# Retention's chunks at a closer spacing, and one more half block's output product in seven products

## The chip, the cores and the metric

The kernel runs on one core of a Trainium2 chip. The metric is the device time of one execution in microseconds (us). Before the change it is 704.63 us, the median of three runs (704.38 to 705.03). The engines of the core work side by side, each on its own queue in order: TensorE (PE in the profile, with its weight loads as PEld), VectorE (DVE), ScalarE (ACT), GpSimd (POOL), and SyncE (SP), which here only starts transfers.

## The reference

Retention over 4 batches, 8 heads, 768 positions and a head size of 64, and on its result a two-layer block with `h - tanh(h)` in its middle:

```python
gamma = 1.0 - 2.0 ** (-5.0 - np.arange(H))
for t in range(S):
    state = gamma[None, :, None, None] * state + np.einsum('bhd,bhe->bhde', k[:, :, t], v[:, :, t])
    y[:, :, t] = scale * np.einsum('bhd,bhde->bhe', q[:, :, t], state)
x = y.transpose(0, 2, 1, 3).reshape(B * S, H * D)     # 3072 x 512
h = x @ w_in                                          # 3072 x 2048
out = (h - np.tanh(h)) @ w_out                        # 3072 x 512
```

## The kernel before

Retention is computed in 24 chunks of 128 positions. The two large products work on 12 half blocks of 256 tokens; the hidden width of 2048 is cut into 8 pairs of 128. A step is one half block `n` with one pair `m2`: an up product (x times w_in), the shrink `h - tanh(h)`, and, two or three steps later, that tile's output product (times w_out). There are 96 steps. The first 8 steps and chunks are in a hand-ordered opening; the loop below starts with step 8. Steps 8 to 31 are of half blocks 0 to 3; from step 32 on each half block has 8 steps in a row, half block 4 from step 32, half block 5 from step 40.

The plain products, and those in seven products (the scheme of Strassen and Winograd: seven products of quarter matrices instead of eight, with sums ahead and behind):

```python
def up(n, m2, i):                                        # L443: 8 calls of 256 columns a step
    for c in range(NC):
        nc.tensor.matmul(hp, w1[:, c, ts(2 * m2 + i, P)], xT[n // 2][:, c, ts(n % 2, TH)], ...)

def down(n, m2, j, first, last):                         # L510: 4 calls of 512 columns a step
    for i in range(2):
        nc.tensor.matmul(o_p[j], gT[n, m2][:, i, ts(j, P)], w2[:, 2 * m2 + i], ...)

def fast_up(n, m2, some):                                # L756: 14 calls of 128 columns a step
    for k in some:
        for c in range(2):
            nc.tensor.matmul(hps[n, m2][:, ts(PLACE[k], P)], s_of[m2][k - 1][:, c],
                             x_of[n][k - 1][:, c], ...)

def fast_products(n, m2, first, last, some):             # L647: 7 calls of 256 columns a step
    for k in some:
        ...
        nc.tensor.matmul(accs[n][k], left[k - 1], right, ...)
```

Each call is two instructions in the profile[...]. The sums that the seven products need are made by GpSimd: `up_weights(m2)` combines quarters of w_in, `up_tokens(n, t)` those of x, `fast_weights(m2)` those of w_out, each in four subtractions or additions, and `fast_sums(n, m2)` those of a tile's shrunk h. Their room is taken from buffers that the conversion of the weights and retention no longer need:

```python
FAST = 5                                   # output product in seven from this half block on
FAST_UP = 4                                # up product in seven from this half block on
def early_room():                          # for up_weights: raw, low, power, and one xT buffer
    ...
    yield xp.tile([P, 4 * BANK], F32, tag="xT", name="fast_x")
def later_room():                          # for fast_weights: retention's v, apart, state and kqT
    ...
```

A chunk of retention needs k and q turned. For chunks 8 and later this is done by transfers: ScalarE splits the words into `apart`, they go to DRAM, and come back transposed as `kqT`:

```python
def turn_by_dma(ci):
    apart = mid.tile([P, 2, 2, H * D], U16, tag="apart", ..., bufs=1)
    for which in range(2):
        nc.scalar.copy(out=apart[:, :, which], in_=words...)                 # L300
    rows = dram.tile([P, 2, 2 * H * D], U16, tag="rows", ...)
    nc.scalar.dma_start(out=rows, in_=apart...)                              # L303
    sides[ci] = mid.tile([P, 2, NP, P], F32, tag="kqT", ...)
    nc.sync.dma_start_transpose(out=sides[ci]..., in_=rows...)               # L305

def products(ci):
    ...  nc.tensor.matmul(..., kh[r, h], vh[r, h], ...)                      # L325, k and v
    ...  nc.tensor.matmul(..., kT[r, p, ts(a, D)], qT[r, p, ts(a, D)], ...)  # L331, needs kqT
```

A step of the loop, with the chunk that may go with it (cut):

```python
FIRST = 8
with_chunk = {BEGUN + 2 * i + 1: FIRST - 3 + i for i in range(NCH - FIRST + 3)}   # BEGUN = 8

def chunk_step(ci):
    if ci >= FIRST:
        outputs_rest(ci)                   # L379, the last part of chunk ci
        keep_x(ci)                         # its result into xT
    ...
    if FIRST <= ci + 2 < NCH:
        products(ci + 2); mask(ci + 2); state(ci + 2)
    load_chunk(ci + 4)
    if not before:
        turn_and_see(ci)                   # turn_by_dma(ci + 3), outputs(ci + 1)
    ...

for s in range(BEGUN, len(steps)):
    ...
    falls_back = s == FALL
    lag = LAG + int(s >= FALL)
    if ci is not None and not falls_back:
        chunk_step(ci)                     # ahead of the step's up product
    for i in with_weights.get(s, []):
        convert(i); load_weights(i + 3)    # weights 12 to 31, up to step 26
    if fast:
        fast_up(n, m2, (1, 5, 7, 6)); up_take(n, m2)
    else:
        for i in range(2):
            up(n, m2, i)
    if falls_back:
        chunk_step(ci)                     # behind it
    ...                                    # shrink, and the output product of an earlier tile
    if s + 1 in with_chunk:
        for which in range(2):
            scale(with_chunk[s + 1] + 3, which, nc.gpsimd)
```

So the words of chunk `ci + 3` are turned in the chunk step of `ci`, and needed by `products` in the chunk step of `ci + 1`.

Of the kernel before, what the change touches and what calls it, by code (L numbers as in the profile page):

```python
# [9 lines left out]
F32 = mybir.dt.float32  # L10
# [6 lines left out]
P = 128  # L17
# [14 lines left out]
def kernel(  # L32
# [27 lines left out]
    NP = H // 2  # L60
# [6 lines left out]
    NCH = NT // P  # L67
    BLK = 4
# [10 lines left out]
    xp = ctx.enter_context(tc.tile_pool(name="xp", bufs=NB - 1))  # L79
# [59 lines left out]
    def load_weights(i):  # L139
        if i >= NW:  # L140
            return
        dst, src = weight_ends(i)
        raw = None
        if w_out.dtype != F32:
            if EARLY <= i < EARLY + 2 * len(rooms):
                raw = rooms[(i - EARLY) // 2][:, (i - EARLY) % 2]
            else:
                raw = stage.tile([P, 2 * BANK], U32, tag="raw", name=f"raw_{i}", bufs=3)
            raws[i] = raw
        if not isinstance(src, list):  # L150
            if raw is None:
                nc.sync.dma_start(out=dst, in_=src)
            else:
                nc.sync.dma_start(out=raw, in_=src.bitcast(U32))
            return
        if raw is not None:
            dst = raw.rearrange("p (c n) -> p c n", c=NC)
        for r, k, w in src:
            nc.sync.dma_start(out=dst[r, k::2], in_=w if raw is None else w.bitcast(U32))
# [46 lines left out]
    def convert(i):  # L206
        convert_begin(i)
        convert_bits(i)
        convert_end(i, nc.gpsimd)
# [18 lines left out]
    xT = {}  # L228
# [186 lines left out]

    def keep_x(ci):
        n, nj = divmod(ci, BLK)
        if nj == 0:
            xT[n] = xp.tile([P, NP, BLK * P], F32, tag="xT", name=f"xT_{n}")

        half = xT[n][:, :, ts(nj // 2, TH)].rearrange("p (n r) t -> p r n t", r=2)
        y = y_banks[:, ci % 2][:, :: 1 - 2 * (ci % 2)]
        for odd in range(2):
            nc.scalar.copy(out=half[:, :, :, ds(P * odd + D * (nj % 2), D)],
                           in_=y[:, :, :, odd::2])
# [10 lines left out]
    def up(n, m2, i):  # L436

        if (n, m2) not in hps:
            hps[n, m2] = bank("h", f"h_{n}_{m2}")
        hp = hps[n, m2][:, ts(i, TH)]  # L440
        keep_busy(hp[:, :P])
        for c in range(NC):
            nc.tensor.matmul(hp, w1[:, c, ts(2 * m2 + i, P)], xT[n // 2][:, c, ts(n % 2, TH)],  # L443
                             start=(i == 0 and c == 0), stop=(c == NC - 1),
                             skip_group_check=True)
# [102 lines left out]

    FAST = 5
    PAIRS = NM // 2
    t_of = {}

# [27 lines left out]
    def fast_weights(m2):  # L582

        b11, b12, b21, b22 = (w2[:, 2 * m2 + i, ts(c, TH)] for i in range(2) for c in range(2))
        t = {k: next(late_room) for k in (2, 3, 4)}
        t[1] = b12
        for k, x, y in ((3, b22, b12), (1, b12, b11), (2, b22, t[1]), (4, t[2], b21)):
            nc.gpsimd.tensor_tensor(t[k], x, y, op=ALU.subtract)
        t_of[m2] = t
# [123 lines left out]
    def end_some(n):  # L713
        for _ in range(min(n, len(ending))):
            ending.pop(0)()
# [7 lines left out]
    FAST_UP = 4  # L723
# [4 lines left out]
    def up_weights(m2):  # L728

        a11, a12, a21, a22 = (w1[:, ds(2 * c, 2), ts(2 * m2 + i, P)]  # L730
                              for i in range(2) for c in range(2))
        s_ = {k: next(up_room).rearrange("p (c m) -> p c m", c=2) for k in (2, 3, 4)}
        s_[1] = a21
        for k, x, y, how in ((3, a11, a21, ALU.subtract), (1, a21, a22, ALU.add),
                             (2, s_[1], a11, ALU.subtract), (4, a12, s_[2], ALU.subtract)):
            nc.gpsimd.tensor_tensor(s_[k], x, y, op=how)
        s_of[m2] = (a11, a12, s_[4], a22, s_[1], s_[2], s_[3])
# [13 lines left out]
    def fast_up(n, m2, some):  # L751
        if 1 in some:
            hps[n, m2] = bank("h", f"h_{n}_{m2}")
# [3 lines that stand above are left out]
                                 x_of[n][k - 1][:, c], start=(k == 1 and c == 0), stop=(c == 1),  # L757
                                 skip_group_check=True)

    def up_take(n, m2):  # L760
        nc.scalar.copy(out=odd_room[0], in_=hps[n, m2])  # L761
# [20 lines left out]
    def downs(lag, half=None):  # L782

        while len(waiting) > lag:
            tile_ = waiting[0] if half == 0 else waiting.pop(0)
            if tile_[0] >= FAST:
                if tile_ == steps[-1]:
# [13 lines left out]
    BEGUN = 8  # L801
# [60 lines left out]


    FIRST = 8
    with_chunk = {BEGUN + 2 * i + 1: FIRST - 3 + i for i in range(NCH - FIRST + 3)}
    with_weights = {BEGUN: [12, 13]}
    for i in range(14, NW):
        with_weights[i - 5] = [i]
# [1 line left out]
    FIRST_UP = steps.index((FAST_UP, 0, True, False))  # L870
    FIRST_DOWN = steps.index((FAST, 0, True, False))
    FALL = FIRST_DOWN + 1
    with_sums = {}
    for m2 in range(PAIRS):
        with_sums.setdefault(FIRST_UP - 4 + m2, []).append(lambda m2=m2: up_weights(m2))
        with_sums.setdefault(FIRST_DOWN + m2, []).append(lambda m2=m2: fast_weights(m2))

    def first_tokens():
# [5 lines left out]
    def more_tokens(n):  # L884
        up_tokens(n, op.tile([P, 4 * TH], F32, tag="sum", name=f"x_{n}"))

    with_sums[FIRST_UP - 2].append(first_tokens)
    for n in range(FAST_UP + 1, 2 * NB):
        at_ = FIRST_UP + 3 + n - FAST_UP if n < FAST_UP + 3 else PAIRS * (n - 1) + 2
        with_sums.setdefault(at_, []).append(lambda n=n: more_tokens(n))  # L890
    before = None

# [6 lines left out]
    def chunk_step(ci):  # L899
        if ci >= FIRST:  # L900
            outputs_rest(ci)
            keep_x(ci)
        middle()
        if before:
            shrink_factors(*before)
            shrink_last_factor(*before)
        if FIRST <= ci + 2 < NCH:
            products(ci + 2)
            mask(ci + 2)
            state(ci + 2)  # L910
        load_chunk(ci + 4)
        if not before:
            turn_and_see(ci)
        elif FIRST <= ci + 1 < NCH - 1:
            outputs(ci + 1)

    def turn_and_see(ci):
        if ci + 3 < NCH:
            turn_by_dma(ci + 3)
        if FIRST <= ci + 1 < NCH - 1:  # L920
            if not before:
                outputs(ci + 1)
            see(ci + 1)

    for s in range(BEGUN, len(steps)):
        n, m2, first, last = steps[s]
        fast = n >= FAST_UP
        ci = with_chunk.get(s)

        falls_back = s == FALL  # L930
        lag = LAG + int(s >= FALL)
        if ci is not None and not falls_back:
            chunk_step(ci)
        for i in with_weights.get(s, []):
            convert(i)
            load_weights(i + 3)
        if fast:
            fast_up(n, m2, (1, 5, 7, 6))
            up_take(n, m2)
        else:  # L940
            for i in range(2):
                up(n, m2, i)
        if falls_back:
            chunk_step(ci)
        if before and ci is not None:
            turn_and_see(ci)
        if ci == NCH - 2:
            outputs(ci + 1)
            see(ci + 1)
        waiting.append(steps[s])  # L950
        if fast:
            if before and ci is None:
                shrink_factors(*before)
                shrink_last_factor(*before)
            up_pairs()
            for make in with_sums.get(s, []):
                make()
            downs(lag, 0)
            fast_up(n, m2, (2, 3, 4))
            up_add(n, m2)  # L960
            shrink_begin(n, m2)
            if before:
                shrink_end(*before)
                if before[0] >= FAST:
                    fast_sums(*before)
            downs(lag, 1)
            end_some(1)
            shrink_two(n, m2)
            before = n, m2
            if s + 1 not in with_chunk:  # L970
                middle()
        else:
            shrink_begin(n, m2)
            shrink_factors(n, m2)
            shrink_multiply(n, m2)
            downs(lag)
            shrink_last_factor(n, m2)
            shrink_end(n, m2)
            for make in with_sums.get(s, []):
                make()  # L980
# [3 lines that stand above are left out]
# [67 lines left out]
```

## Time and profile before

| | before |
|---|---|
| time, median of three runs | 704.63 us |
| span of the profiled run | 703.4 us |
| mean granted TensorE clock in it | 0.999 |
| TensorE busy | 694.7 us (99%) |
| VectorE busy | 514.7 us (73%) |
| ScalarE busy | 432.6 us (61%) |
| GpSimd busy | 345.7 us (49%) |

Busy time is the time in which an instruction of the engine runs; the shares are of the span. Matmuls are pipelined, so that their printed lengths overlap; the distance from one start to the next tells what one costs. In a timeline the columns are the start in us from the span's start, the length in us, the engine, the line, the operation, what is written and read, and the number of instructions merged; in brackets is idle time ahead of it and what ended it.

### The profile page before, as it was taken

What the parts mean: (1) busy time and instruction counts of PE and PEld (TensorE: products, weight loads), DVE (VectorE), ACT (ScalarE), POOL (GpSimd) and SP (SyncE); (2) the same over time, 40 slices, a digit from 0 to 9 for tenths busy, and PEclk for the clock granted to TensorE, in tenths of its full rate; (3) what the DMA queues carried; (4) which work ended last, traced back from release to release, by engine and by line L of the source; (5) the groups of instructions that cost most, each with busy time, mean ns of one, the idle gap of its engine ahead of it and who ended that gap; (6) DMA issues with size and microseconds to landing.
All of it is one profiled execution on the core that took longest, in us unless ns stands there. A gap on an engine that the chain in (4) does not pass through costs nothing.

```text
span 703.4 us, 16524 instructions
## 1 busy us (share of the span) xinstructions
PE 694.7 (99%) x6554; PEld 571.1 (81%) x6554; DVE 514.7 (73%) x882; ACT 432.6 (61%) x818; POOL 345.7 (49%) x491
## 2 busy tenths in 40 slices
PE   8999999999999999999999999999999999999997
PEld 7886666666777666776789999999999999999996
DVE  4898878987888756667667776676677676776765
ACT  4677657777677655566666555556665555666553
POOL 1464444545454662575288853354453544544333
PEclk9999999999999999999999999999999999999999
DMA  8781537867666455464200000000000000000001
GB/s 229 213 240 55 134 98 203 202 189 197 165 178 157 126 156 138 135 165 107 62 32 1 1 2 16 16 1 31 1 0 32 1 1 31 2 16 16 1 16 46
DMA packets 119678, 59.97 MB, mean 85 GB/s; under 512 B 101808, under 2 KB 112688, under 8 KB 119600
## 3 DMA queue, kind: packets, MB, share of 16 engines
q1 hardware_dynamic: 117008, 50.21, 27.5%
q10 hardware_dynamic: 2592, 8.69, 3.1%
q8 instruction: 52, 0.85, 0.5%
q14 instruction: 26, 0.21, 0.1%
HBM read 35.83 MB, written 14.68 MB: 72 GB/s over the span
## 4 chain that ended last, share of the span: by engine, by line
PE 93%; DVE 2%; DMA 1%; ACT 1%; issue 1%; SPq 1%; POOL 0%; POOLq 0%; DVEq 0%; ACTq 0%
PE h L756 28%; PE o L510 19%; PE h L443 15%; PE fast_t L647 8%; PE fast_o L647 7%; PE y L647 7%; PE y L379 3%; PE s L331 1%; PE s L325 1%; PE h_early L443 1%; PE kqTp L276 1%; DMA raw<-in_moe_w_in_dram 1%; DMA q<-in_q_dram 1%; PE h_early L217 0%; SPq L240 0%
## 5 line engine op out<-in xcount | busy, mean ns | idle before, releaser
L510 PE MATMUL o<-w,g 128*128 128x512 f32 x320 | 145.3, 593 | 0.0
L456 ACT ACTIVATE th<-h 128x512 f32<-128x512 f32 x64 | 38.2, 598 | 136.0 <-DVE h L773 133.5
L443 PE MATMUL h<-xT,w 128*128 128x256 f32 x480 | 110.7, 382 | 0.0
L598 POOL TENSOR_TENSOR s<-g 128x128 f32<-128x128 f32 x56 | 25.7, 458 | 164.2 <-DVE g L502 160.3
L443 PEld LDWEIGHTS h<-xT,w 128*128 128x128 f32 x480 | 89.7, 190 | 18.9 <-issue 6.9
L510 PEld LDWEIGHTS o<-w,g 128*128 128x128 f32 x320 | 59.1, 190 | 55.0 <-issue 51.9
L502 DVE COPY_PREDICATED g<-large,th 128x512 f32<-128x512 int32 x96 | 85.4, 889 | 9.4
L200 POOL TENSOR_TENSOR low<-low,power 128x512 f32<-128x512 f32 x30 | 38.8, 1294 | 104.6 <-DVE power L192 79.2
L756 PEld LDWEIGHTS h<-xT,w 128*128 128x128 f32 x512 | 76.5, 191 | 14.0 <-issue 7.2
L771 DVE TENSOR_TENSOR h<-h,fast_head 128x256 f32<-128x256 f32 x64 | 27.7, 433 | 72.6 <-PE h L756 67.6
L481 DVE TENSOR_TENSOR th<-h,th 128x512 f32<-128x512 f32 x94 | 64.1, 682 | 22.0 <-ACT th L454 20.7
L756 PE MATMUL h<-xT,w 128*128 128x128 f32 x512 | 78.6, 276 | 0.2 <-ACT fast_head L761 0.2
L462 ACT ACTIVATE q<-u,tab 128x512 f32<-128x512 f32 x96 | 69.8, 727 | 1.7
L494 DVE SCALAR_TENSOR_TENSOR g<-q,h 128x512 f32<-128x512 f32 x64 | 44.0, 688 | 34.9 <-ACT q L470 33.2
L470 ACT ACTIVATE q<-u,tab 128x512 f32<-128x512 f32 x96 | 69.5, 723 | 0.0
L471 ACT ACTIVATE large<-u,tab 128x512 f32<-128x512 f32 x96 | 68.6, 714 | 0.0
L485 DVE SCALAR_TENSOR_TENSOR h<-q,h 128x512 f32<-128x512 f32 x94 | 64.9, 690 | 4.8 <-ACT q L462 4.6
L756 PE MATMUL h<-x,w 128*128 128x128 f32 x448 | 68.3, 275 | 0.0
L766 POOL TENSOR_TENSOR fast_head<-fast_head 128x256 f32<-128x256 f32 x64 | 47.0, 734 | 43.5 <-ACT fast_head L761 43.5
L756 PEld LDWEIGHTS h<-x,w 128*128 128x128 f32 x448 | 59.0, 192 | 0.0
L761 ACT COPY fast_head<-h 128x512 f32<-128x512 f32 x64 | 37.5, 585 | 26.2 <-PE h L756 25.4
L501 DVE TENSOR_TENSOR g<-g,u 128x512 f32<-128x512 f32 x64 | 47.8, 747 | 0.0
(196 smaller groups left out, 1418.2 us busy)
## 6 DMA issues: line engine op xcount, KB each, us to landing
rows<-apart ACTq DMA_DIRECT2D x16, 512.0 KB, 4.0
k<-in_k_dram SPq DMA_DIRECT2D x24, 256.0 KB, 4.0
v<-in_v_dram SPq DMA_DIRECT2D x24, 256.0 KB, 5.1
raw<-in_moe_w_out_dram SPq DMA_DIRECT2D x12, 512.0 KB, 4.0
out_dram<-sum SPq DMA_DIRECT2D x22, 256.0 KB, 2.0
q<-in_q_dram SPq DMA_DIRECT2D x16, 256.0 KB, 4.6
raw<-in_moe_w_in_dram SPq DMA_DIRECT2D x14, 256.0 KB, 4.2
raw<-in_moe_w_in_dram SPq DMA_DIRECT2D x28, 128.0 KB, 4.0
```

Source lines behind the costliest of these rows:

```text
L443: nc.tensor.matmul(hp, w1[:, c, ts(2 * m2 + i, P)], xT[n // 2][:, c, ts(n % 2, TH)], start=(i == 0 and c == 0), stop=(c == NC - 1), skip_g ...
L462: nc.scalar.activation(q0, shrinking[n, m2][0], AF.Square, bias=bias0)
L470: nc.scalar.activation(q1, u, AF.Square, bias=bias1, scale=math.sqrt(A))
L471: nc.scalar.activation(large, u, AF.Relu, bias=bias_m)
L481: nc.vector.tensor_tensor(th, hp, th, op=ALU.subtract)
L485: nc.vector.scalar_tensor_tensor(hp, in0=shrinking[n, m2][2], scalar=C0, in1=hp, op0=ALU.add, op1=ALU.mult)
L501: nc.vector.tensor_tensor(flat, src, u, op=ALU.mult)
L502: nc.vector.copy_predicated(flat, large.bitcast(I32), th)
L510: nc.tensor.matmul(o_p[j], gT[n, m2][:, i, ts(j, P)], w2[:, 2 * m2 + i], start=(first and i == 0), stop=(last and i == 1))
L647: nc.tensor.matmul(accs[n][k], left[k - 1], right, start=first and k in (1, 6, 7, 4), stop=last, skip_group_check=True)
L756: nc.tensor.matmul(hps[n, m2][:, ts(PLACE[k], P)], s_of[m2][k - 1][:, c], x_of[n][k - 1][:, c], start=(k == 1 and c == 0), stop=(c == 1), ...
L766: nc.gpsimd.tensor_tensor(odd_room[1], first[:, :2], first[:, 3:1:-1], op=ALU.add)
```

## The change

It puts the output product of half block 4 into seven products too (`FAST = 4`). That needs the combinations of w_out at step 32 instead of 40, and so the room that retention holds; so the chunks are spaced one and a half steps apart instead of two, every second one behind its step's up product instead of ahead of it. The combinations of w_in are made three steps earlier, the buffer of x's first block is handed on after that of the second, and half block 6's token sums are made later.

```diff
     def keep_x(ci):
         n, nj = divmod(ci, BLK)
-        if nj == 0:
-            xT[n] = xp.tile([P, NP, BLK * P], F32, tag="xT", name=f"xT_{n}")
+        if n not in xT:
+            for i in (1, 0) if n == 0 else (n,):
+                xT[i] = xp.tile([P, NP, BLK * P], F32, tag="xT", name=f"xT_{i}")
...
-    FAST = 5
+    FAST = 4
...
-    with_chunk = {BEGUN + 2 * i + 1: FIRST - 3 + i for i in range(NCH - FIRST + 3)}
+    with_chunk = {BEGUN + 1 + 3 * i // 2: FIRST - 3 + i for i in range(NCH - FIRST + 3)}
+    behind_up = {BEGUN + 1 + 3 * i // 2 for i in range(1, NCH - FIRST + 3, 2)}
...
-        with_sums.setdefault(FIRST_UP - 4 + m2, []).append(lambda m2=m2: up_weights(m2))
+        with_sums.setdefault(FIRST_UP - 7 + m2, []).append(lambda m2=m2: up_weights(m2))
         with_sums.setdefault(FIRST_DOWN + m2, []).append(lambda m2=m2: fast_weights(m2))
...
-        at_ = FIRST_UP + 3 + n - FAST_UP if n < FAST_UP + 3 else PAIRS * (n - 1) + 2
+        at_ = FIRST_UP + 4 if n == FAST_UP + 1 else PAIRS * (n - 1) + 2
...
-        falls_back = s == FALL
+        falls_back = s == FALL or s in behind_up
...
-        if falls_back:
+        if falls_back and ci is not None:
             chunk_step(ci)
```

`FALL` is the second step of the first half block with seven output products: step 41 before, step 33 after. Chunks 5 to 23 go with steps 9, 11, 13 to 45 before, and with 9, 10, 12, 13, 15, 16 to 36 after; those with 10, 13, 16 and so on to 34, and the one with step 33, stand behind the up product.

## The prediction

> **What bounds the kernel now.** I read the page first, parts 1 and 4, then the chain of waits of TensorE, and then TensorE's timeline at four places.
>
> ```profile
> PE 694.7 (99%) x6554; PEld 571.1 (81%) x6554; DVE 514.7 (73%) x882; ACT 432.6 (61%) x818; POOL 345.7 (49%) x491
> ...
> PE 93%; DVE 2%; DMA 1%; ACT 1%; issue 1%; SPq 1%; POOL 0%; POOLq 0%; DVEq 0%; ACTq 0%
> ```
>
> TensorE is busy for 99% of the span and 93% of the chain that ended last runs through it; no other engine is near. A busy share alone would not settle it, so I also looked at who TensorE waits for. Its longest single waits (1.1 us on ScalarE's "seen" copies, 1.1 us on VectorE's first memset) add up to about 5 us in all, nearly all in the first 60 us. From 92 us on its instructions follow each other at fixed distances. So the time is a sum of TensorE's work, and a change is worth what it takes out of TensorE's queue less the waits that it puts in.
>
> The unit of work before 281 us is a step of 6.89 us (up product 3.45, output product 3.43). Where a retention chunk goes with it, the timeline shows:
>
> ```profile
> 143.85 0.46 PE L379 MATMUL y<-a,v 64*64 64x64 f32 x16
> 144.13 0.65 PE L325 MATMUL s<-v,k 64*64 64x64 f32 x32
> 144.60 0.65 PE L331 MATMUL s<-kqT 64*64 64x64 f32 x32
> 145.08 0.69 PE L379 MATMUL y<-kqT,state 64*64 64x64 f32 x32
> 145.59 0.41 PE L379 MATMUL y<-a,v 64*64 64x64 f32 x16
> 145.94 3.72 PE L443 MATMUL h<-xT,w 128*128 128x256 f32 x16
> 149.50 3.60 PE L510 MATMUL o<-w,g 128*128 128x512 f32 x8
> 152.93 3.62 PE L443 MATMUL h<-xT,w 128*128 128x256 f32 x16
> 156.38 3.60 PE L510 MATMUL o<-w,g 128*128 128x512 f32 x8
> 159.91 0.46 PE L379 MATMUL y<-a,v 64*64 64x64 f32 x16
> ```
>
> The columns are start, length, engine, line, operation. From chunk to chunk it is 159.91 - 143.85 = 16.06 us, that is 2 x 6.89 + 2.28: a chunk costs TensorE 2.28 us wherever it stands. (The printed lengths overlap, because matmuls are pipelined; I take starts.)
>
> **What the Trainium skill says.** "Perfetto Trace Analysis", Identifying the Most-Contended Engine, says that matmul busy share is a poor measure of TensorE's headroom because of pipelining; this trace agrees (the lengths above overlap by 0.17 to 0.2 us), which is why I count from start to start. "DMA: Bandwidth & Descriptors", Issuing engines are not separate DMA queues, says that transfers started by ScalarE and by SyncE share the same 16 DMA engines and interleave. The trace agrees: a chunk's words go to DRAM (rows<-apart, 512 KB) in 3.0 us at 294 us, where no weights come in any more, but in 3.8 to 5.4 us before 275 us. The same page, Two DMAs through the same engine are not ordered, says that a dependent transfer has to wait for the completion count of the first. The kernel does so: the transpose back (kqT<-rows) is issued 0.02 to 0.08 us after the rows have landed, so the two latencies add.
>
> **The change, part by part.** (1) FAST from 5 to 4: half block 4, that is 8 steps, has its output product in seven products of 256 columns instead of four of 512. Its up product is in seven already, before and after. The cost of such a step before, and of one of a half block that has both in seven:
>
> ```profile
> 296.32 0.61 PE L756 MATMUL h<-xT,w 128*128 128x128 f32 x4
> ...
> 302.98 0.40 PE L379 MATMUL y<-a,v 64*64 64x64 f32 x12
> ```
>
> A step starts at 296.32 and the next chunk follows at 302.98; 0.09 us of that belong to the switch to 64-wide products (the last product before a chunk lasts 0.52 us instead of 0.43). So the step costs 6.66 - 0.09 = 6.57 us. Later:
>
> ```profile
> 376.41 0.71 PE L756 MATMUL h<-xT,w 128*128 128x128 f32 x4
> ...
> 382.66 0.61 PE L756 MATMUL h<-xT,w 128*128 128x128 f32 x4
> ...
> 388.81 0.61 PE L756 MATMUL h<-xT,w 128*128 128x128 f32 x4
> ```
>
> 388.81 - 382.66 = 6.15 us. The saving is 8 x (6.57 - 6.15) = 3.3 us, all of it on TensorE. This is close to one eighth of the 3.43 us that an output product costs (0.43 us).
>
> (2) The 19 chunks that remain go with steps 9, 10, 12, 13, ... 36 instead of 9, 11, 13, ... 45. That takes no work from TensorE: 19 x 2.28 us before and after. It is there so that retention's buffers are free for the combinations of w_out by step 32 instead of 40. But it shortens the time that each chunk's trip has. Between the start of ScalarE's copies for a chunk and the products that need the turned words lies exactly one distance of chunks. Before that is 16.06 us; after it is 1.5 x 6.89 + 2.28 = 12.6 us, 3.45 us less. Placing every second chunk behind the up product makes both distances equal.
>
> How much slack was there? From copies to landing it takes 10.2 to 11.7 us for chunks 11 to 19. The landings lie 4.1 to 5.5 us ahead of the product that needs them (L331). Less 3.45 us leaves 0.6 to 2.0 us if the latency stays the same. From chunk 20 on no weights are loaded and the trip takes 9.0 to 9.4 us: no wait. But the first trip, chunk 8's, is different:
>
> ```profile
> 104.50 0.35 ACTq L303 DMA_DIRECT2D rows<-apart  x1
> 108.41 2.05 SPq L305 DMA_TRANSPOSE kqT<-rows  x1
> 109.50 3.60 PE L510 MATMUL o<-w,g 128*128 128x512 f32 x8
> 113.03 0.69 PE L325 MATMUL s<-v,k 64*64 64x64 f32 x32
> 113.54 0.65 PE L331 MATMUL s<-kqT 64*64 64x64 f32 x32
> ```
>
> The transpose issued at 108.41 lands 4.4 us later, at 112.8, and L331 starts at 113.54: 0.7 us to spare. After, this chunk goes with step 10 behind its up product, that is ahead of the output product that starts here at 109.50. Nothing that leads to the landing is moved by the change: up to there all queues keep their order (the program's order says so). So L331 comes up at 109.5 + 0.5 = 110.0 and waits until 112.8: 2.8 us of TensorE's time, once. Chunk 9's trip (0.1 us to spare before) gains from this wait and from its scaled q coming a step earlier; I count nothing for it.
>
> (3) GpSimd's work moves forward: combinations of w_in from steps 28 to 35 to steps 25 to 32, those of w_out from 40 to 47 to 32 to 39. A pair of weights costs it 4 x about 0.8 = 3.2 us either way, a chunk's two scalings 2 x 1.04 to 1.5 us, a conversion of weights 2 x 1.28. In step 26 that is 3.2 + 2.6 + 2.6 = 8.4 us against 6.89, in the steps around it 3 to 6. From step 33 it is 0.73 + 3.2 + 4 x 0.46 = 5.8 us of a step of 6.15, as in steps 41 to 47 before, where TensorE lost under 1 us. New is that one set of token differences (4 x 0.74 = 3 us) falls in step 36.
>
> (4) The turned order of xT_1 and xT_0 and the later tokens of half block 6 only say which buffer comes free when; no time.
>
> The sum: -3.3 (seven products) + 2.8 (chunk 8) + about 0.5 (other late trips) - 0.3 (part of the 0.8 us lost between 349 and 360 us that a less crowded start of half block 5 may spare) = -0.3 us. From 704.63 that is 704.3 us.
>
> **The rivals.** (a) No wait appears, because the transpose of chunk 8 lands earlier than in this one profile or because I have misplaced the product: the time is 704.6 - 3.3 = 701.3 us. For it speaks that the later distances are plainly chosen to fit; against it the 112.8 us above. (b) The trip becomes the bound in the whole weights stretch. The DMA engines carry 170 GB/s at a busy share of 0.64 between 113 and 274 us; the same chunks' bytes in 12.6 instead of 16.06 us add some 15%. If each trip grows by 1 us, about every second of ten chunks (a wait gives the next trip as much more time) waits up to 1 us, 3 to 5 us in all, and the time is 707 to 709 us. For it: transposes of 5.8 and 5.9 us stand among those of 4.2. (c) GpSimd becomes the bound in steps 32 to 39. Each pair of sums for an up product must be there within about 3 us, or the two h banks are not free for the next product but one. With the 3 us of tokens in step 36 this could cost 1 to 3 us: 705 to 707 us. Against it: GpSimd idles 2.0 and 1.4 us between sums even in this stretch before.
>
> **Range and chances.** 704.3 us in the middle; down to 701.3 if (a) is right; (b) and (c) together reach 708. As 8 times in 10 I take 701.3 to 707.6. A gain of 2% would be 14 us, four times what the seven products can save; a loss of 2% would need every trip to be late by over 1.5 us. So faster 0.01, within 2% 0.98, slower 0.01.
>
> **What would show it.** Right: steps 35 to 42 at 6.15 us; 320 instructions of L510 become 256; TensorE waits some 2.8 us for a transpose at about 110 us, at the products with kqT; few and short waits there later; chunks 12.6 us apart. Wrong: no wait at 110 us (then a), waits of L331 in most chunks up to 250 us (b), or GpSimd's sums at the head of TensorE's or VectorE's waits in steps 32 to 40 (c). The prediction fails if an engine other than TensorE ends the waits in a whole stretch.

## The result, and the profile after

The changed kernel takes 709.72 us (median of 6 runs, 709.16 to 712.07) against 704.89 us of the kernel before in runs beside it: a ratio of 1.0077, with a 95% interval of 1.006 to 1.0094. It is slower by 4.8 us; the prediction had 704.3 us and a range up to 707.6.

The lines of the page that answer to those shown of before (in the changed kernel the lines of the source stand one further down: L444 is the plain up product, L511 the plain output product, L757 and L648 the up and output products in seven):

```profile
PE 693.0 (98%) x6602; PEld 580.2 (82%) x6602; DVE 518.1 (73%) x888; ACT 432.3 (61%) x818; POOL 356.0 (50%) x523
...
PE 80%; DMA 4%; ACT 4%; POOL 4%; DVE 3%; SPq 2%; issue 2%; POOLq 0%; ACTq 0%; DVEq 0%
```

TensorE is still busy for 98% of the span, and a reader who stops there sees nothing. The second line tells: the chain that ended last ran through TensorE for 93% before and for 80% now. Transfers, ScalarE and GpSimd had 2% of it and now have 12%. That share is not the loss, but it says where to look. TensorE's view of whom it waited for names the places:

```profile
PE s L331 <- DMA kqT<-rows: 3.0, 3, 2.3
PE y L379 <- ACT xT L425: 2.9, 2, 1.7
...
PE h L757 <- ACT fast_head L762: 0.8, 1, 0.8
```

(The columns are us in total, times, longest.) A wait stands here only where TensorE had run dry, so that the sums are too small. To size them I took, all along TensorE's queue, the distance of two starts less the usual distance at that place. The profiled run of the changed kernel then lost

| where | what TensorE waited for | after | before |
|---|---|---|---|
| 110 us, step 10 | turned words of chunk 8 | 2.47 | 0 |
| 125 us, step 12 | turned words of chunk 9 | 0.61 | 0 |
| 176 and 264 us | turned words of chunks 13 and 20 | 0.70 | 0 |
| 309 us, step 34 | ScalarE's copy of chunk 22 | 1.92 | 0 |
| 338 to 359 us, steps 38 to 41 | sums of an up product | 1.48 | 0 |
| elsewhere from 300 to 360 us | | 0.13 | 0.81 |
| the opening, up to 58 us (the difference alone) | | 0.32 | 0 |

That is 6.8 us more, less the 3.3 us of the seven products: 3.5 of the 3.9 us by which the span grew (703.4 to 707.3). The other 0.4 us lie in distances too small to name. For the waits from 338 us on the expectations below say steps 36 to 39: what starts them is GpSimd's work of step 36, and TensorE itself waits in steps 38 to 41.

The first two places in TensorE's timeline of the changed kernel:

```profile
106.37 3.62 PE L444 MATMUL h<-xT,w 128*128 128x256 f32 x16
109.91 0.69 PE L325 MATMUL s<-v,k 64*64 64x64 f32 x32
112.91 0.69 PE L331 MATMUL s<-kqT 64*64 64x64 f32 x32 [2.30 <-DMA kqT<-rows]
113.53 3.70 PE L511 MATMUL o<-w,g 128*128 128x512 f32 x8
```

```profile
308.39 0.46 PE L379 MATMUL y<-a,v 64*64 64x64 f32 x16
310.56 0.69 PE L379 MATMUL y<-kqT,state 64*64 64x64 f32 x32 [1.71 <-ACT xT L425]
311.08 0.41 PE L379 MATMUL y<-a,v 64*64 64x64 f32 x16
```

The bracket is TensorE's idle time ahead of the instruction and what ended it. At 110 us the products of k and v are done and those with kqT stand. At 308 us the next chunk's outputs wait for ScalarE to copy the last chunk out of the same banks; ScalarE comes to this copy at 309.83 us, behind three other operations, the first of which VectorE had held up until 308.39 us. The seven products do what they are for. Half block 4's steps, from here to the next line, are 6.14 us apart, where 6.57 us were needed before:

```profile
329.19 0.61 PE L757 MATMUL h<-xT,w 128*128 128x128 f32 x4
...
335.33 0.61 PE L757 MATMUL h<-xT,w 128*128 128x128 f32 x4
```

The third place is best seen in the chain that ended last, between 330 and 340 us (start, length, what):

```profile
330.65 1.17 POOL x L747
...
331.89 2.11 POOL x L747 x3
334.00 0.42 POOL s L599
334.49 0.46 POOL s L600
334.95 0.41 POOL s L601
335.36 0.42 POOL s L602
335.78 0.70 POOL fast_head L767
336.50 0.44 DVE h L772
...
342.23 0.69 POOL fast_head L767
```

TensorE is not in it at all. The token sums of half block 5 (L747) hold up the sums of an output product (L599 to L602), these the sum of an up product (L767), and that holds up VectorE, ScalarE and the bank that TensorE needs at 339.76 us. The last line shows why the delay doesn't die out: from one L767 to the next GpSimd takes 6.45 us, without waiting for anyone, and TensorE's work in a step takes 6.14. So TensorE comes to this place at 339.76, 346.21, 352.67 and 359.08 us, some 6.45 us apart, and loses 0.91, 0.19, 0.21 and 0.16 us.

### The profile page after: what moved, and what is told of

It is laid out like the page before. It is cut to its first block, busy times and chain, and to the rows that moved or that the text cites. A ratio compares the mean times of both kernels' runs of the same rounds, so it can differ in the third digit from the quotient of the medians.

```text
span 707.3 us, 16646 instructions
## 1 busy us (share of the span) xinstructions
PE 693.0 (98%) x6602; PEld 580.2 (82%) x6602; DVE 518.1 (73%) x888; ACT 432.3 (61%) x818; POOL 356.0 (50%) x523
## 4 chain that ended last, share of the span: by engine, by line
PE 80%; DMA 4%; ACT 4%; POOL 4%; DVE 3%; SPq 2%; issue 2%; POOLq 0%; ACTq 0%; DVEq 0%
PE h L757 26%; PE o L511 12%; PE h L444 12%; PE y L648 8%; PE fast_t L648 8%; PE fast_o L648 7%; PE y L379 3%; DMA kqT<-rows 2%; PE s L331 1%; DMA raw<-in_moe_w_in_dram 1%; PE s L325 1%; SPq L245 1%; ACT apart L300 1%; SPq L159 1%; DMA raws<-in_moe_w_in_dram 1%
## 5 line engine op out<-in xcount | busy, mean ns | idle before, releaser
L599 POOL TENSOR_TENSOR s<-g 128x128 f32<-128x128 f32 x64 | 29.3, 458 | 189.5 <-DVE g L503 189.5
L511 PE MATMUL o<-w,g 128*128 128x512 f32 x256 | 116.1, 596 | 0.0
L444 PE MATMUL h<-xT,w 128*128 128x256 f32 x480 | 110.2, 382 | 0.0
L444 PEld LDWEIGHTS h<-xT,w 128*128 128x128 f32 x480 | 90.1, 190 | 20.6 <-issue 8.9
L511 PEld LDWEIGHTS o<-w,g 128*128 128x128 f32 x256 | 47.5, 190 | 47.5 <-issue 44.0
L757 PEld LDWEIGHTS h<-xT,w 128*128 128x128 f32 x512 | 76.7, 191 | 11.0 <-ACT fast_head L762 2.4
L757 PE MATMUL h<-xT,w 128*128 128x128 f32 x512 | 78.4, 276 | 0.8 <-ACT fast_head L762 0.8
L757 PE MATMUL h<-x,w 128*128 128x128 f32 x448 | 68.3, 275 | 0.0
L757 PEld LDWEIGHTS h<-x,w 128*128 128x128 f32 x448 | 59.0, 192 | 0.0
L767 POOL TENSOR_TENSOR fast_head<-fast_head 128x256 f32<-128x256 f32 x64 | 46.8, 731 | 8.2 <-ACT fast_head L762 8.2
```

Of the source, the lines that this page charges most:

```text
L767: nc.gpsimd.tensor_tensor(odd_room[1], first[:, :2], first[:, 3:1:-1], op=ALU.add)
```

## The experiments

Theory A was that three separate places carry the loss, each with a wait of its own. Its main rival B was that the closer spacing makes everything slower, so that a wait removed in one place comes back in another. The ratios are to the kernel before, run on the same chip.

| run | ratio | 95% interval |
|---|---|---|
| the changed kernel | 1.0077 | 1.006 to 1.0094 |
| changed_again | 1.0073 | 1.0055 to 1.009 |
| spacing_only | 1.016 | 1.0137 to 1.0182 |
| chunk22_later | 1.0068 | 1.0054 to 1.0082 |
| tokens_early | 1.0041 | 1.0028 to 1.0053 |
| both_seam | 1.0026 | 1.0018 to 1.0033 |
| first_trips | 1.002 | 1.0013 to 1.0027 |
| trips_and_chunk22 | 1.0009 | 1.0002 to 1.0017 |
| trips_and_tokens | 0.9998 | 0.9988 to 1.0008 |
| seam_and_trips | 0.9982 | 0.9973 to 0.9991 |
| seam_and_earlier_trip | 0.999 | 0.998 to 1.0001 |
| all_and_scales | 0.997 | 0.9958 to 0.9982 |
| filled_wait | 1.006 | 1.0048 to 1.0073 |

### The spacing without the seven products

```diff
-    FAST = 4
+    FAST = 5
```

> The change without its seven products: FAST stays 5, the chunks keep the new spacing. Theory A (three separate places, each with its own wait: the first two trips of turned words, ScalarE's late copy of chunk 22 in step 34, GpSimd's sums in steps 36 to 39): the first trips still cost 3.1 us and the later ones some 0.8, the sums of step 36 no longer fall together with those of w_out, and half block 4's output products come back with 3.3 us; chunk 22's wait stays at 0 to 1.9 us: 708 to 711 us, that is 3.5 to 6 us above the kernel before. Theory B (the closer spacing makes every stage a little slower, by load on the DMA engines and on the queues): waits spread over all chunks between 110 and 310 us, the same total. Rival C (the cost comes from the seven products and their sums alone): equal to the kernel before within 1 us.

It took 715.8 us, worse than any theory had it. The profiled span is 714.8 us. Its losses against the kernel before: 1.4 us in the opening, 2.3 us at 111 us, 1.6 us at half clock behind that (a granted TensorE clock of 0.5, see the last section), 1.1 us of later trips, 1.1 us at 314 us for ScalarE's copy, and 4.1 us between 362 and 416 us, most of it in this line:

```profile
383.73 0.71 PE L757 MATMUL h<-xT,w 128*128 128x128 f32 x4 [2.08 <-ACT fast_head L762]
```

The expectation missed that with FAST at 5 the combinations of w_out go back to steps 40 to 47, and that the change has moved half block 6's token sums to step 42, into the middle of them. So the same collision on GpSimd comes up with another half block. Rival C, that the seven products and their sums alone cost the time, falls: less these 4.1 us the run would still be some 6 us slower than the kernel before. The run isn't a clean half of the change, since it brings in a collision that the changed kernel doesn't have.

### Chunk 22 one step later

```diff
+    with_chunk[35] = with_chunk.pop(34)
+    behind_up.discard(34)
     with_weights = {BEGUN: [12, 13]}
```

> The changed kernel with chunk 22 moved from step 34 (behind the up product) to step 35 (ahead of it). Theory A: the wait of 1.9 us at 308.6 us is ScalarE coming late to the copy of chunk 22, because step 33 with its chunk lies right before and has no output product to fill the time; with a step between it goes: 1.5 to 1.9 us less than the changed kernel, 707.8 us. Theory B: the wait moves to another place, less than 0.5 us gained.

The wait of 1.92 us is gone from the trace; 0.34 us stand in the next step instead. But the time, 709.81 us, is not 707.8: the ratio fell from 1.0077 to 1.0068 only, with intervals that overlap. In the profiled run TensorE ran at half clock for 6.8 us behind the wait at 110 us, which cost 3.0 us, more than the edit gives. So this run alone doesn't decide; the edit had to be tried without that wait (below).

### Half block 5's token sums five steps earlier

```diff
-        at_ = FIRST_UP + 4 if n == FAST_UP + 1 else PAIRS * (n - 1) + 2
+        at_ = FIRST_UP - 1 if n == FAST_UP + 1 else PAIRS * (n - 1) + 2
```

> The changed kernel with the token sums of half block 5 made in step 31 instead of 36, where GpSimd is idle for 7.8 us. Theory A: GpSimd's queue in steps 36 to 39 is 3 us shorter, the four waits of the up products for ScalarE's copy there (0.91, 0.19, 0.21 and 0.16 us) go: 1.3 to 1.5 us less, 708.2 us. Theory B: no more than 0.3 us, since VectorE or ScalarE would end these waits just as late.

708.6 us (ratio 1.0041 against 1.0077). All four waits between 338 and 360 us are gone, and nothing came in their place: behind chunk 22's wait, which ends at 310 us, no distance is over the usual one by more than the 0.1 us that follow every chunk. The sums now stand where GpSimd had nothing to do, from 289.19 to 292.12 us, and it still idles 4.4 us behind them. GpSimd's dense steps are still there (6.3 to 6.5 us each, from 332.61 us on), but now it enters them with 1.0 us to spare. B's claim that VectorE or ScalarE would be as late falls. By the ratios the gain is 2.5 us, more than the 1.5 us of waits; the part of the clock in that is not known, and `trips_and_tokens` below sizes this edit better.

### The first trips

```diff
-    D10 v6 D11 v7 ... g7 E5 W12 L8 W13 W14
+    D10 v6 D11 v7 ... g7 E5 W12 L8 W13 W14 s8 w8
...
         for i in with_weights.get(s, []):
             convert(i)
-            load_weights(i + 3)
+            if s not in behind_up:
+                load_weights(i + 3)
...
         if falls_back and ci is not None:
             chunk_step(ci)
+        if s in behind_up:
+            for i in with_weights.get(s, []):
+                load_weights(i + 3)
...
-        if s + 1 in with_chunk:
+        if s + 1 in with_chunk and s > BEGUN:
             ...scale(with_chunk[s + 1] + 3, which, nc.gpsimd)
```

> The changed kernel with chunk 8's scaling put at the end of the opening and, in steps with a chunk behind the up product, the next load of weights issued behind the chunk's loads. Theory A: chunk 8's words are sent 3 to 4 us earlier and chunk 9's transpose no longer queues behind loads of weights: 2.5 to 3.1 us less than the changed kernel, 706.8 us, and no wait over 0.5 us for kqT before 130 us. Theory B: the transfers only change places, under 1 us gained.

706.64 us, as expected (ratio 1.002), though 1.16 us of wait for chunk 8 stay where under 0.5 were expected: ScalarE sends the words 4.0 us earlier (100.84 instead of 104.83 us), but they now travel beside loads of weights and of chunk 9, and rows and transpose take 10.5 us together instead of 8.0. Chunk 9 no longer waits. In the changed kernel its rows had landed at 116.48 us and SyncE came to the transpose at 119.81 us:

```profile
108.43 2.07 SPq L305 DMA_TRANSPOSE kqT<-rows  x1
110.61 6.30 SPq L159 DMA_DIRECT2D raw<-in_moe_w_in_dram  x6
...
118.29 1.42 SPq L245 DMA_DIRECT2D v<-in_v_dram  x1
119.81 3.05 SPq L305 DMA_TRANSPOSE kqT<-rows  x1
```

The second line is two loads of weights; the second stood from 112.5 to 115.2 us, until its buffer was free. Everything behind it in SyncE's queue stood too. So it isn't transfer time alone that made a trip late, but the order in which one engine starts transfers.

### The edits together

> Chunk 22 in step 35 and the token sums of half block 5 in step 31, together. Theory A (separate waits that add): no wait over 0.4 us between 300 and 365 us; 1.9 + 1.5 us less than the changed kernel's undisturbed 709.2, that is 705.8 us, and up to 2.5 us more in executions where TensorE's clock halves behind the wait of 2.5 us at 110 us. Theory B (one wait hides another): at most 2 us less.

Both edits of the seam, where retention ends and half block 4's seven products begin (chunk 22 and the token sums): ratio 1.0026, that is 0.0051 x 705 = 3.6 us less than the changed kernel; 3.4 had been expected. Of the waits between 300 and 365 us 0.73 and 0.20 us stay, the first more than expected.

> The two edits of the seam and those of the first trips, together. Theory A: what is left of the first trips is 1.2 us; 705.8 - 2 = 703.8 us, with the clock at 1.000 since no wait is over 1.5 us. Theory B: 706 us or more.

With the first trips as well: ratio 0.9982 (704.58 us; the kernel before takes 706.04 on this chip). The loss has turned into a gain of 1.3 us. This is for theory A and against B: the gains nearly add (0.0051 and 0.0057 of the time alone, 0.0095 together).

> The edits of the first trips and chunk 22 in step 35, without the early token sums. Theory A: 1.9 us less than the first trips alone (ratio 1.002 to the kernel before), less 0.4 us that come back in the step after: ratio 0.9993 to 1.0005; the four waits between 338 and 360 us (1.4 us) stay. Theory B: no less than the first trips alone.

> The edits of the first trips and the early token sums, chunk 22 left in step 34. Theory A: 1.4 us less than the first trips alone, ratio 1.000; the wait of 1.9 us at 307 us stays, and with it half clock behind it in some executions. Theory B: no less than the first trips alone.

These two give each edit of the seam by itself, where the wait at 110 us is short. Chunk 22: 1.002 to 1.0009, or 0.8 us; 1.1 to 1.9 us were expected, and of the wait of 1.9 us 0.9 us came back in the steps after (0.75 and 0.20 us). With the token sums early besides, the same edit gives 1.1 us (0.9998 to 0.9982); the intervals overlap both times, and it is the shorter wait in the traces that shows the gain. The token sums: 1.002 to 0.9998, or 1.6 us; 1.4 us were expected. With chunk 22 left in place the 2.05 us at 307 us stay.

> As the one before, and chunk 5's step, which sends chunk 8's words, is step 8 instead of 9; GpSimd scales q and v of a chunk ahead of the combinations of w_in that stand in the same step. Theory A: chunk 8's words land before 106 us, no wait there; chunk 20's trip is 3 us shorter; what stays are 0.5 to 1 us of late trips in the weights stretch: 701.6 to 702.8 us, that is faster than the kernel before by 2 to 3 us. Theory B: the shorter distance keeps costing 3 us or more: 705 us or slower.

Here chunk 5 goes with step 8 (`with_chunk[8] = with_chunk.pop(9)`) and GpSimd scales ahead of the combinations. Chunk 8's words landed at 102.3 us and no longer waited, but chunk 10's did, for 1.13 us: 704.69 us on the chip where seam_and_trips has 704.58, with a wide spread (703.26 to 708.77). A miss: ahead of chunk 10's trip ScalarE waited 2.71 us for the scaled q, which GpSimd made behind a conversion of weights, and sent the rows 4.8 us after it had begun on them (2.0 us in seam_and_trips).

> The changed kernel itself, beside the three below on the same chip. All theories: 4 to 5.5 us above the kernel before, ratio 1.006 to 1.008; waits of TensorE at the same three places (110 to 125, 308, 338 to 359 us), and half clock for 3.4 or 6.8 us behind one of the long waits in some executions.

> All edits of the first trips and of the seam, and GpSimd scales a chunk's q and v ahead of the combinations of w_in that stand in the same step. Theory A: chunk 20's trip loses the 3.6 us that ScalarE waited for the scaled q, its wait of 0.4 us goes: ratio to the kernel before 0.9975. Theory B: the order on GpSimd changes nothing, ratio 0.998 or more.

The changed kernel once more has 1.0073. The last version is seam_and_trips with this besides, and chunk 5 back in step 9:

```diff
             shrink_end(n, m2)
-            for make in with_sums.get(s, []):
-                make()
         if s + 1 in with_chunk and s > BEGUN:
             for which in range(2):
                 scale(with_chunk[s + 1] + 3, which, nc.gpsimd)
+        if not fast:
+            for make in with_sums.get(s, []):
+                make()
```

703.25 us beside 705.55 of the kernel before and 710.74 of the changed one: ratio 0.997 (0.9958 to 0.9982), 0.3% below the kernel before and 1.1% below the changed one. ScalarE sends chunk 20's rows 2.2 us after it begins on them instead of 5.6, and they no longer hold TensorE up. The step from 0.9982 to 0.997 is itself within the noise of the two runs. The chain that ended last is TensorE's again:

```profile
PE 91%; SPq 2%; DVE 2%; DMA 2%; ACT 1%; issue 1%; POOL 0%; POOLq 0%; DVEq 0%; ACTq 0%
```

Of the 3.3 us that the seven products save 2.1 us (0.003 x 705) are kept; the longest waits that are left are 0.89 us at 110 us and 0.69 us at 307 us.

### The wait filled with work

```diff
+        if ci == 6:
+            idle[0] = 11
         if FIRST <= ci + 2 < NCH:
             products(ci + 2)
```

> The changed kernel with chunk 22 in step 35, and eleven products of zeros on TensorE ahead of chunk 8's products, which fill most of its wait of 2.5 us with work that nothing reads. If the half clock seen in some executions behind this wait is brought on by TensorE's idleness: the same time as the best executions without the filling, 707.2 to 708.9 us, a clock of 0.999 or more, and a spread under 1 us. If it has another cause: a spread of 3 us and clocks of 0.995 as without it (708.75 to 712.57).

On top of chunk22_later, eleven products of zeros stand ahead of chunk 8's products. They compute nothing that is read. The granted clock is 0.999 or 1.0 in all six runs, where five of six without the filling had 0.995 to 0.997. So in these runs the half clock came with the idle time and not without it. The time isn't better for it: ratio 1.006 against 1.0068, 709.18 to 711.51 us. The zeros take 2.55 us of TensorE's queue; other waits in its profiled run are longer (1.25 us for chunk 13). Its spread of 2.3 us missed the expectation of under 1 us, so that the half clock is not the only thing that spreads these times.

## Why the prediction was wrong

**The seven products: right.** A step without waits takes 6.14 us (6.15 predicted), so that 8 x 0.42 us are saved, and L511 has 256 instructions.

**The first trip: right, and the neighbour missed.** 2.8 us were predicted for chunk 8, 2.47 measured (2.67 when the changed kernel ran again). For chunk 9 "I count nothing" stood, on the ground that the wait ahead of it helps. It waited 0.61 us, since SyncE reached its transpose 3.3 us after the words had landed. The working took the landing of the rows for the start of the transpose, which in the kernel before was true to 0.1 us.

**The other trips: right in sum, in part by luck.** 0.5 us predicted, 0.70 measured: 0.41 for chunk 13 and 0.29 for chunk 20. For chunk 20 "no wait" stood, with a trip of 9.0 to 9.4 us; it took 12.3 us, as ScalarE waited 3.35 us for the q that GpSimd scales behind the sums of step 26, the very step of 8.4 us of the working. The rival that the trip becomes the bound in the weights stretch fell: between 113 and 250 us the DMA share rose from 0.67 to 0.81, the trips of chunks 11 to 19 grew by only 0.4 us on the mean (11.1 to 11.5 us), and in the table two late ones stand.

**GpSimd and the seam: the step that failed.** The sum had -0.3 us for the stretch from 300 to 360 us. Measured are +2.7 us (3.5 of waits against 0.8), which is 3.0 of the 5.1 us between the forecast change of the time (-0.3) and the measured one (+4.8). It has two parts.

Chunk 22, 1.92 us. The prediction gave the chunks a price of 2.28 us "wherever it stands". The 19 prices are right only while something lies between a chunk's last part and the next chunk's outputs that covers ScalarE's copy. In the middle of retention these are the products of the next chunk but one; chunk 22 has none, as there are 24 chunks. In the kernel before, the up product of its step lay between:

```profile
362.07 0.46 PE L379 MATMUL y<-a,v 64*64 64x64 f32 x16
362.47 0.71 PE L756 MATMUL h<-xT,w 128*128 128x128 f32 x4
...
364.45 0.69 PE L379 MATMUL y<-kqT,state 64*64 64x64 f32 x32
```

After, both stand behind the up product with nothing between (308.39 and 310.56 us above). One step later, the chunk stands ahead of an up product again; that took half of the wait away where the first trips were mended too, and saved 0.8 us. What the step before it, which has no output product, adds to the wait was not tried by itself.

The token sums, 1.48 us. Rival (c) named this place and gave it 1 to 3 us, and was then left out of the middle on the ground that GpSimd idled in this stretch before. It did, for 2.0 and 1.4 us between sums; 3 us more don't fit into that. These sums are not new in step 36: they stood there before too, and what the change brings to the step is the combinations of w_out. And the working's 5.8 us for GpSimd in a step of 6.15 were too little: where its work is dense it takes 6.45 us a step, since of the four subtractions for w_out one takes 1.26 us and one 1.07 us instead of 0.73. The kernel before had such steps as well (6.47 us from 359.72 us on), but in steps 43 and 45 a chunk gave GpSimd time, and it idled there for 1.7 and 1.1 us. With the closer spacing no chunk comes after step 36, so that a delay stays until the combinations end with step 39.

A slip on which nothing rests: the 1.1 us given as a longest single wait on the "seen" copies is the sum of two, the longer of 0.7 us.

**The half clock: not in the prediction.** It explains a part of what the median lies above the profiled run: the changed kernel's six runs are 709.2 to 709.3 us at a clock of 0.999 or 1.0, and 710.1, 711.5 and 712.1 us at 0.995 or 0.996.

What stays open: why chunk22_later gains only 0.6 us where the trace shows 1.5 us less waiting, and why filled_wait is no faster although its clock is full.

## What to carry to other kernels

Where one engine sets the time, price a rearrangement by its first and last members, not by the middle: in the middle each wait is covered by a neighbour that the ends do not have. And when work moves to another step, compare the engine's measured time for the dense steps that follow with the step of the engine that sets the time: here 6.45 us against 6.14, so that a delay was not caught up, and TensorE lost another 0.2 us in each step until the work ended. When several waits are found, remove them together as well as one by one; here no single edit brought the kernel below the one before, and all together turned a loss of 0.8% into a gain of 0.3%.

## What the runs showed of the hardware that was not expected

A wait of about 2 us on TensorE can be paid twice. Behind the wait at 110 us, changed_again ran at half clock (columns of the windows: stretch, us, busy times of the five, granted clock, DMA share, GB/s):

```profile
109.00:113.40 4.40, 1.91 (x41) 1.33 (x39) 4.16 (x6) 3.85 (x6) 4.32 (x4) 0.98 0.86 155
113.40:117.00 3.60, 3.60 (x36) 2.19 (x37) 3.46 (x7) 3.13 (x7) 1.53 (x2) 0.55 0.76 264
117.00:120.00 3.00, 3.00 (x11) 1.70 (x10) 2.84 (x5) 1.08 (x2) 1.56 (x2) 1.00 0.85 220
```

```profile
114.44 4.77 PE L511 MATMUL o<-w,g 128*128 128x512 f32 x8
119.05 3.62 PE L444 MATMUL h<-xT,w 128*128 128x256 f32 x16
```

The same eight L511 took 3.70 us in the first profile of this kernel. The half clock lasted 3.4 us here and, at 0.5, cost some 1.5 us: from the first product with kqT to the next up product it is 5.67 us instead of 4.16. It lasted 6.8 us in chunk22_later, 3.4 us in spacing_only, and 3.4 us behind the waits at 307 us of 1.94 us in first_trips and 2.05 us in trips_and_tokens. Whether it comes differs from one execution to the next: the first profile of the changed kernel has the waits of 2.47 and 1.92 us and no half clock. "TensorE: Matmul & The Clock Gate", HAM oscillation, in the Trainium skill, gives idle gaps of over some 3.4 us as what brings it on; the measurements decide, and here 1.9 to 2.7 us were enough at times. With the wait at 110 us filled, the mean clock was 0.999 or more in six runs of six.
